# Global queries of four heads in the partitions of one tile, and transposes and products with V of neighbouring units in one gap

## The chip, the cores and the metric

The kernel runs on one core of a Trainium2 chip. The metric is device time in microseconds (us). Engines are named as the profile names them: PE (TensorE; PEld is its loading of weights), DVE (VectorE), ACT (ScalarE), POOL (GpSimd) and SP (which issues the DMAs).

## What is computed

An attention with local and global tokens, and a gated feed-forward layer on its output. There are 8 batches, 8 heads, 512 local and 32 global tokens, and 64 columns a head; the feed-forward has 512 columns in and out and 1536 hidden ones.

```python
k_all, v_all = concat([k_g, k_l]), concat([v_g, v_l])
out_g = softmax(q_g @ k_all.T / 8) @ v_all            # global queries see all keys
s_ll = where(abs(i - j) <= 32, q_l @ k_l.T / 8, -1e9) # local ones a window
out_l = softmax(concat([q_l @ k_g.T / 8, s_ll])) @ concat([v_g, v_l])
x = concat([out_g, out_l]).reshape(4352, 512)         # heads side by side
y = (sigmoid(x @ w_gate) * (x @ w_val)) @ w_out
```

The feed-forward weights arrive as float64 words and are converted on the chip.

## The kernel before

The tokens go through in chunks. Chunks 0 and 1 are halves of batch 0 (256 local tokens each), chunks 2 to 8 are one batch each (512 local tokens); a last feed-forward chunk takes the 256 global tokens of all batches. While the feed-forward of one chunk runs on PE, the attention of the next is put between its matmuls; from chunk 2's feed-forward on this is a steady alternation; beside the feed-forward of chunk 8 and of the global tokens no attention runs.

Numbers are kept to near float32: a float32 operand is split into two float32r parts, and a product takes three passes (high by high, low by high, high by low). In `ffn_stream` one step handles 128 hidden columns f of a chunk: twelve matmuls of 512 tokens into `bank_g`, twelve into `bank_v`, and twelve of the step before into four output banks `bank_o`. A **tick** is four such matmuls, so a step has nine ticks and a chunk 108. After each tick the generator yields, and all events of the queue that are due are issued; an event's number in the list (-1 to 9) decides between events of one tick. The recording layer may then still move instructions within each engine.

`att_events` puts the attention of a chunk in the queue. A head has two local units of two 128-query blocks each (one in the half chunks), and, where the chunk has global queries (chunks 1 to 8), one global unit of its 32 queries: 64 global units in all. Units follow each other every `PER` = 4 ticks (1.1 in chunk 1, 3 in chunk 2), and a unit has four stages, at 0, 3, 6 and 9 ticks of its start (scaled by a quarter of the spacing in chunks 1 and 2):

- stage 0: scores on PE into `bank_x` (L225; global: L299 into `bank_x`, L301 into `bank_y`), masking or maximum on DVE, exponential on ACT (L240; global: L308, L309);
- stage 1: reciprocal of the sum and scaling on DVE (into `p_buf`, or `pg_buf` for global units);
- stage 2: transposes on PE into `bank_y` (L254: four of 128x128; global L317: five of 32x128), a copy on ACT and the low part on DVE (`pt` L264; `ptg` L324);
- stage 3: products with V on PE into `bank_x` (L280 and L281; global L330), then copy on ACT, sum on DVE, sum on POOL into `x32` (L285; global `xg32`, L337).

`x_split` then makes the two parts of the feed-forward's input. Chunks 0 and 1 and the first four heads of chunk 2 are *native*: q, k and v stay float32 and are not split. All of `bank_g`, `bank_v`, `bank_x` and `bank_y` rotate through four of the eight banks of PSUM (`tag="att", bufs=4`). `vhl` holds V of a head in two parts, in two buffers. In ticks -2 to 45 the weights are converted (`convert`: DVE, ACT and POOL), beside the two half chunks and the first heads of chunk 2.

Of the kernel before, what the change touches and what calls it, by code (L numbers as in the profile page):

```python
# [17 lines left out]
P = 128  # L18
# [26 lines left out]
# the engines that share a kind of operation in turn: v(ector), s(calar)  # L45
# [9 lines left out]
def kernel(ctx, tc, qk, v, w_gate, w_val, w_out, out_l, out_g):  # L55
# [21 lines left out]
    # window column c < 96 stands for key c - 32, c >= 128 for key c - 64  # L77
    # (relative to the block's first query); the columns between are global
# [15 lines left out]
    pg = const.tile([32, 5 * P], F32, name="pg_buf")  # L94
# [24 lines left out]
    def convert(i, hi, lo):  # L119
        """The two float32r parts of a float64 [128, KT or 1, n] block, given as words."""  # L120
        src = w_src[i]
        t, n = src.shape[1], src.shape[2] // 2
        st, v = (o[i % len(o)].rearrange("p (t n) -> p t n", t=t) for o in conv_bufs)
        words = st.rearrange("p t (n two) -> p t n two", two=2)
        low, high = words[:, :, :, 0], words[:, :, :, 1]
        vf, hf = v.bitcast(F32), high.bitcast(F32)
        with tc.issue_after(anchor[0].ins) if i < 3 else nullcontext():
            nc.vector.tensor_scalar(v, high, 0x80000000, None, op0=ALU.bitwise_and)
# [6 lines left out]
            nc.vector.scalar_tensor_tensor(v, low, 29, v, op0=ALU.logical_shift_right, op1=ALU.bitwise_or)  # L135
            nc.vector.scalar_tensor_tensor(v, high, 3, v, op0=ALU.logical_shift_left, op1=ALU.bitwise_or)
# [35 lines left out]
    def load_v(T):  # L172
        c, n = T["wins"], T["n"]
        if T["native"]:
            nw = c.stop
            ng = 16 // nw
            if T["h"] % ng == 0:
                t = spl.tile([P, ng, nw, D], F32, name="v_nat", tag="vhl")
                nc.sync.dma_start(t, v[n:n + ng, :, c].rearrange("n p j d -> p n j d"))
                T["group"]["v"] = t  # L180
# [19 lines left out]
    def split_v(T):  # L200
# [3 lines left out]
        vhl = spl.tile([P, 8, 2 * D], F32R, name="vhl")  # L204
# [11 lines left out]
    def local_unit(T, blocks, x32s, h, col0):  # L216
# [35 lines left out]
        for i in range(2):  # L252
            for t in range(2):
                nc.tensor.transpose(pt_ps[:, 2 * i + t], pb[:, i, t * P:(t + 1) * P], ident)  # L254
        if nat:
# [31 lines left out]
    def global_unit(T, b, h):  # L287
# [3 lines left out]
        prow, kt = 64 * (h % 2), h // 2  # L291
        qg = ks[0][:, QK - SG - q0:QK - q0]
        sa = ps.tile([32, 4, P], F32, name="bank_x", tag="att", bufs=4)
        sb = ps.tile([32, 32], F32, name="bank_y", tag="att", bufs=4)
        for half in range(2):
# [4 lines left out]
        for t, (src, k0) in enumerate(zip(ks, k0s)):  # L300
            nc.tensor.matmul(sb, qg, src[:, k0 + 96:k0 + 128], start=t == 0, stop=t == last)  # L301
        mg = small.tile([32, 4], F32, name="mg")
        saf = sa.rearrange("p a c -> p (a c)")
        nc.vector.tensor_reduce(mg[:, 0:1], saf, axis=AX.X, op=ALU.max)
        nc.vector.tensor_reduce(mg[:, 1:2], sb, axis=AX.X, op=ALU.max)
        nc.vector.tensor_scalar(mg[:, 2:3], mg[:, 0:1], mg[:, 1:2], -0.125, op0=ALU.max, op1=ALU.mult)
        sg = small.tile([32, 2], F32, name="sg")
        nc.scalar.activation(pg[:, 0:512], saf, AF.Exp, bias=mg[:, 2:3], scale=0.125, accum_out=sg[:, 0:1])  # L308
        nc.scalar.activation(pg[:, 544:576], sb, AF.Exp, bias=mg[:, 2:3], scale=0.125, accum_out=sg[:, 1:2])  # L309
        yield  # L310
        nc.vector.tensor_scalar(mg[:, 3:4], sg[:, 0:1], sg[:, 1:2], 1e-9, op0=ALU.add, op1=ALU.add)
        nc.vector.reciprocal(mg[:, 3:4], mg[:, 3:4])
        scaled(0, pg[:, 0:576], pg[:, 0:576], mg[:, 3:4])
        yield
        pt_ps = ps.tile([P, 5, 32], F32, name="bank_y", tag="att", bufs=4)
        for j in range(5):
            nc.tensor.transpose(pt_ps[:, j], pg[:, j * P:(j + 1) * P], ident[0:32, 0:32])  # L317
        if nat:
            pt = att.tile([P, 5, 32], F32, name="ptg_nat", tag="ptg", bufs=1)
            nc.scalar.copy(pt, pt_ps)  # L320
        else:
            pt = att.tile([P, 5, 64], F32R, name="ptg", bufs=1)
            nc.scalar.copy(pt[:, :, 0:32], pt_ps)
            nc.vector.tensor_tensor(pt[:, :, 32:64], pt_ps, pt[:, :, 0:32].bitcast(F32), op=ALU.subtract)  # L324
        yield
        vt = T["v"]
        xg = xg32[prow:prow + 64, kt, b * SG:(b + 1) * SG]
        o_ps = ps.tile([64, 32] if nat else [P, 64], F32, name="bank_x", tag="att", bufs=4)
        for j in range(5):
            nc.tensor.matmul(o_ps, vt[:, (VM + VS)[j], :], pt[:, j, :], start=j == 0, stop=j == 4)  # L330
        if nat:
            nc.scalar.copy(xg, o_ps)
            return
        y = att.tile([64, 64], F32, name="y", bufs=1)
        nc.scalar.copy(y, o_ps[64:128])
        nc.vector.tensor_tensor(y, o_ps[0:64], y, op=ALU.add)
        nc.gpsimd.tensor_tensor(xg, y[:, 0:32], y[:, 32:64], op=ALU.add)  # L337

# [70 lines left out]
    # ---- driver: attention of the next chunk runs between the matmul groups  # L409
    def att_events(ci, start, per, tail=0):  # L410
        """(tick, order, thunk) of all attention work for chunk ci."""
# [19 lines left out]
        def adv(h, i):  # L431
            if (h, i) not in gens:
                gens[h, i] = (local_unit(heads[h], blocks[2 * i:2 * i + 2], x32s, h, 2 * i * P) if i < nu
                              else global_unit(heads[h], b, h))
# [3 lines left out]
        for h in range(NH):  # L438
# [30 lines left out]
    # the first two half chunks share the steps in which the weights are converted  # L469
# [7 lines left out]
    # events on the feed-forward's clock: one tick is four 512-token matmuls  # L477
# [23 lines left out]
    queue.sort(key=lambda e: e[:2])  # L501
# [9 lines left out]
def host_layout(inputs):  # L511
# [11 lines left out]
    for j in range(4):  # L523
# [7 lines left out]
        ve[:, VS[j], 32:64] = vg  # L531
        if j < 3:
# [31 lines left out]
```

## Time and profile before

| | |
|---|---|
| median of three runs | 1266.6 us (1265.78 to 1267.1) |
| profiled execution, its span | 1265.6 us |
| mean granted clock of PE | 0.986 |
| attention of chunk 0 before the first feed-forward matmul | to 49.7 us |
| outputs of the two half chunks | from 272.2 us |
| outputs of chunks 2 to 6 start at | 418.4, 557.6, 696.8, 835.9, 975.1 us |
| outputs of chunks 7, 8 and of the global tokens start at | 1113.6, 1211.3, 1260.9 us |

The times of outputs show the steady part: 139.1 to 139.2 us from chunk to chunk with attention beside the feed-forward, 97.7 us without. In the profile's lines `bank_x<-pt,vhl` reads "written from"; the number behind it is that of instructions, then busy us and mean ns of one, then the engine's idle time before them with what ended it. Matmuls overlap, so what a block of them costs is read from start to start in the timeline, not from the mean.

### The profile page before, as it was taken

The page shows a single profiled execution, that of the slowest core. Times are in us where ns is not written, and L with a number is a line of the kernel's source. Part 1 is how long each engine was busy: PE and PEld are TensorE (multiplying, and loading weights), DVE is VectorE, ACT ScalarE, POOL GpSimd, SP SyncE. Part 2 cuts the span into 40 slices and gives each one's busy share as a digit, 9 for nine tenths or more (in the row PEclk, how much of TensorE's full clock was granted, in tenths as well). Part 3 has the DMA queues.
Part 4 walks back from the last instruction along what each step waited for, and adds up shares of the span by engine and source line. Part 5 has one row for each costly group of instructions (what it writes and reads, how often), then busy time and mean ns, then how long its engine had stood idle before and what let it go on. Part 6 is the DMA issues. An engine that isn't in the chain of part 4 may idle for free.

```text
span 1265.6 us, 20474 instructions
## 1 busy us (share of the span) xinstructions
PE 1221.5 (97%) x6820; PEld 994.1 (79%) x6820; DVE 877.6 (69%) x2433; ACT 783.3 (62%) x1899; POOL 570.6 (45%) x573
## 2 busy tenths in 40 slices
PE   5899989999999999999999999999999999999998
PEld 4676768788788877888788877888788877888897
DVE  4797976757877777857876778767775787632232
ACT  4586766756666666666666667756765766532233
POOL 1444554545555355545555455535554555311111
PEclk9698999999999999999999999999999999999999
DMA  5576864333333333333333423343334332122143
GB/s 198 197 259 225 254 191 145 92 121 99 92 107 98 115 99 108 91 121 108 107 92 107 126 78 107 109 127 111 92 86 126 116 92 87 44 90 67 67 133 117
DMA packets 59497, 151.90 MB, mean 120 GB/s; under 512 B 6144, under 2 KB 19456, under 8 KB 59392
## 3 DMA queue, kind: packets, MB, share of 16 engines
q1 hardware_dynamic: 59392, 150.59, 38.9%
q8 instruction: 54, 0.88, 0.3%
q14 instruction: 51, 0.42, 0.1%
HBM read 135.36 MB, written 15.20 MB: 119 GB/s over the span
## 4 chain that ended last, share of the span: by engine, by line
PE 77%; DVE 13%; ACT 5%; issue 3%; POOL 1%; DMA 1%; SPq 0%; POOLq 0%; DVEq 0%; ACTq 0%
PE bank_g L362 20%; PE bank_v L362 19%; PE bank_o L396 19%; PE bank_x L225 5%; PE bank_y L254 4%; DVE p_buf L213 3%; DVE th L378 2%; PE bank_y L317 2%; PE bank_x L330 2%; PE bank_x L280 2%; PE bank_x L299 2%; PE bank_x L281 1%; DVE pg_buf L213 1%; ACT s_sb L240 1%; DVE pt L264 1%
## 5 line engine op out<-in xcount | busy, mean ns | idle before, releaser
L362 PE MATMUL bank_g<-xt,wg 128*128 128x512 f32 (+1 forms) x1440 | 340.3, 371 | 1.8 <-DVE th L380 1.8
L362 PE MATMUL bank_v<-xt,wv 128*128 128x512 f32 (+1 forms) x1440 | 332.6, 368 | 3.0 <-DVE pt L264 2.7
L396 PE MATMUL bank_o<-wo,hh 128*128 128x512 f32 x1224 | 334.0, 404 | 0.8 <-ACT hh L382 0.4
L362 PEld LDWEIGHTS bank_g<-xt,wg 128*128 128x128 f32 x1440 | 238.6, 192 | 41.6 <-issue 3.4
L362 PEld LDWEIGHTS bank_v<-xt,wv 128*128 128x128 f32 x1440 | 237.8, 190 | 40.7 <-PE bank_y L301 3.1
L396 PEld LDWEIGHTS bank_o<-wo,hh 128*128 128x128 f32 x1224 | 214.1, 189 | 38.9 <-ACT hh L382 1.2
L383 POOL TENSOR_TENSOR hh<-th,hh 128x512 fp32r<-128x512 f32 (+1 forms) x120 | 137.6, 1147 | 199.7 <-ACT hh L382 198.8
L240 ACT ACTIVATE s_sb<-s_sb,nm 128x224 f32<-128x224 f32 x240 | 113.8, 475 | 143.1 <-DVE nm L237 142.0
L213 DVE TENSOR_SCALAR p_buf<-s_sb,r 128x128 f32<-128x128 f32 (+1 forms) x443 | 151.8, 386 | 4.2 <-PE bank_y L254 0.4
L375 DVE TENSOR_SCALAR mn<-bank_g 128x512 f32<-128x512 f32 (+1 forms) x108 | 67.3, 623 | 110.7 <-ACT th L370 109.3
L378 DVE SCALAR_TENSOR_TENSOR th<-th,mn 128x512 f32<-128x512 f32 (+1 forms) x120 | 101.5, 846 | 59.0 <-ACT mn L376 52.7
L285 POOL TENSOR_TENSOR x<-t 64x256 f32<-64x256 f32 x104 | 76.4, 734 | 142.8 <-DVE t L284 138.7
L194 POOL TENSOR_TENSOR kl<-qk_raw,qk_hi 128x704 fp32r<-128x704 f32 x52 | 88.4, 1701 | 114.8 <-ACT qk_hi L193 114.8
L370 ACT ACTIVATE th<-bank_g 128x512 f32<-128x512 f32 (+1 forms) x120 | 63.5, 529 | 97.7 <-PE bank_g L362 96.1
L382 ACT CAST hh<-th 128x512 fp32r<-128x512 f32 (+1 forms) x120 | 66.5, 554 | 68.1 <-DVE th L380 67.3
L237 DVE CUSTOM_DVE_ANT_0 s_sb<-bank_x,masks 128x224 f32<-128x224 f32 x240 | 83.8, 381 | 12.7 <-PE bank_x L225 8.4
L254 PE MATMUL bank_y<-ident,p_buf 128*128 128x128 f32 x496 | 80.1, 282 | 10.8 <-DVE p_buf L213 6.6
L196 POOL TENSOR_TENSOR qk_hi<-qk_raw,qk_hi 64x256 fp32r<-64x256 f32 x104 | 87.7, 863 | 4.1
L254 PEld LDWEIGHTS bank_y<-ident,p_buf 128*128 128x128 f32 x496 | 60.9, 143 | 32.5 <-ACT pg_buf L308 6.6
L243 DVE TENSOR_SCALAR r<-sm 128x2 f32<-128x2 f32 x128 | 29.3, 229 | 75.5 <-ACT s_sb L240 74.2
L193 ACT CAST qk_hi<-qk_raw 128x1248 fp32r<-128x1248 f32 x52 | 64.1, 1233 | 22.2 <-PE bank_y L301 22.1
L380 DVE TENSOR_TENSOR th<-bank_v,th 128x512 f32<-128x512 f32 (+1 forms) x120 | 72.4, 604 | 5.1 <-PE bank_v L362 1.3
(109 smaller groups left out, 1985.9 us busy)
## 6 DMA issues: line engine op xcount, KB each, us to landing
wo<-wo_dram SPq DMA_DIRECT2D x116, 512.0 KB, 3.5
qk_raw<-in_qk_dram SPq DMA_DIRECT2D x104, 312.0 KB, 4.4
v_raw<-in_v_dram SPq DMA_DIRECT2D x52, 256.0 KB, 2.6
out_dram<-ob SPq DMA_DIRECT2D x34, 256.0 KB, 3.0
xt<-in_w_gate_dram SPq DMA_DIRECT2D x12, 512.0 KB, 4.5
xt<-in_w_val_dram SPq DMA_DIRECT2D x12, 512.0 KB, 4.4
xt<-in_w_out_dram SPq DMA_DIRECT2D x12, 512.0 KB, 4.9
v_nat<-in_v_dram SPq DMA_DIRECT2D x8, 512.0 KB, 5.5
```

The source lines that it names most:

```text
L194: nc.gpsimd.tensor_tensor(kl, t[:, K0:Q1], hi[:, K0:Q1].bitcast(F32), op=ALU.subtract)
L196: nc.gpsimd.tensor_tensor(hi[64:128, r], t[64:128, r], hi[64:128, r].bitcast(F32), op=ALU.subtract)
L213: nc.vector.tensor_scalar(out, in_, by, None, op0=ALU.mult)
L237: anchor[0] = nc.vector.tensor_tensor_reduce(out=s_sb[:, i], in0=s_ps[:, i, 0:WIN], in1=masks[:, m], scale=-0.125, scalar=3.0e38, op0=ALU. ...
L240: nc.scalar.activation(s_sb[:, i], s_sb[:, i], AF.Exp, bias=nm[:, i:i + 1], scale=-1.0, accum_out=sm[:, i:i + 1])
L254: nc.tensor.transpose(pt_ps[:, 2 * i + t], pb[:, i, t * P:(t + 1) * P], ident)
L285: nc.gpsimd.tensor_tensor(dst, t0[:, :, 0], t0[:, :, 1], op=ALU.add)
L362: nc.tensor.matmul(acc, w[a][:, t, fs], xt[:, c, t, x0:x0 + ntok], start=n == 0, stop=n == 11)
L378: nc.vector.scalar_tensor_tensor(th, th, 1.0, mn, op0=ALU.add, op1=ALU.mult)
L380: nc.vector.tensor_tensor(th, acc, th, op=ALU.mult)
L383: nc.gpsimd.tensor_tensor(hh[:, 1, 0:ntok], th, hh[:, 0, 0:ntok].bitcast(F32), op=ALU.subtract)
L396: nc.tensor.matmul(o_ps[t], ph[:, a, t * P:(t + 1) * P], pwo[:, c], start=f2 == 0 and i == 0, stop=f2 == NF - 1 and i == 2)
```

## The change

Four things change.

- **Global units of four heads share one tile.** `pg` has 128 partitions instead of 32. At each head's stage 0 ACT copies the raw scores (32x512 and 32x32) into rows 32(h mod 4) of `pg`. The first three heads of four end there. At the fourth, one maximum, one exponential, one scaling over 128 partitions x 544 columns, five transposes of 128x128 (into two banks), one copy and one low part for each bank, and then, in one stage, the 20 products with V (five of each head, as before) into one bank, with one sum for all four. The 32 global keys move from columns 544 to 575 to columns 96 to 127, ahead of the local ones, so the host puts V of the global tokens in the matching rows of a window of V that was empty there.
- **Stages.** The copies after the transposes become a stage of their own, and products with V come at 6 + `PER` ticks instead of 9. So they fall on the tick of the transposes of the next unit. `STAGES` now has pairs of ticks and orders: on one tick the transposes (2) go first, then the products of the unit before (3), then the copies of the new transposes (4). `x_split` follows one tick later.
- **Buffers of V.** `vhl` and `v_nat` have five buffers instead of two, since V of four heads is kept until the group's products. The room for software-issued DMAs is set to 512 bytes, which makes place for it; all DMAs of the kernel are issued by SP.
- Event times are rounded to six digits before they are sorted, and the scores against the global keys are issued ahead of those against the local ones.

PE, one local unit to the next, in the steady part, before (`pt` and `vhl` are the products with V, `p_buf` the transposes, `bank_g` the feed-forward):

```order
L301 MATMUL bank_y<-kl,qk_hi 32x32
L362 MATMUL bank_g<-xt,wg_111 128x512 x4
L280 MATMUL bank_x<-pt,vhl 128x256
L281 MATMUL bank_x<-pt,vhl 128x256
L280 MATMUL bank_x<-pt,vhl 128x256
L281 MATMUL bank_x<-pt,vhl 128x256
L362 MATMUL bank_g<-xt,wg_112 128x512 x4
L254 MATMUL bank_y<-ident,p_buf 128x128 x4
L362 MATMUL bank_g<-xt,wg_111 128x512 x4
```

and in the changed kernel, at a place of the same kind:

```order
L308 MATMUL bank_x<-kl,qk_hi 32x4x64
L379 MATMUL bank_g<-xt,wg_111 128x512 x4
L379 MATMUL bank_g<-xt,wg_112 128x512 x4
L261 MATMUL bank_y<-ident,p_buf 128x128 x4
L288 MATMUL bank_x<-pt,vhl 128x256
L289 MATMUL bank_x<-pt,vhl 128x256
L288 MATMUL bank_x<-pt,vhl 128x256
L289 MATMUL bank_x<-pt,vhl 128x256
L379 MATMUL bank_g<-xt,wg_111 128x512 x4
```

The products have moved behind the transposes of the next unit, and two ticks of the feed-forward now stand together ahead of them.

PE at the transposes of a global unit (`pg_buf`), before, of one head:

```order
L280 MATMUL bank_x<-pt,vhl 128x256
L281 MATMUL bank_x<-pt,vhl 128x256
L362 MATMUL bank_v<-xt,wv_113 128x512 x4
L317 MATMUL bank_y<-ident,pg_buf 128x32 x5
L396 MATMUL bank_o_4958<-wo,hh 128x512
```

and in the changed kernel, of four heads:

```order
L379 MATMUL bank_v<-xt,wv_113 128x512 x4
L329 MATMUL bank_y<-ident,pg_buf 128x128
L329 MATMUL bank_x<-ident,pg_buf 128x128 x4
L288 MATMUL bank_x<-pt,vhl 128x256
L289 MATMUL bank_x<-pt,vhl 128x256
L288 MATMUL bank_x<-pt,vhl 128x256
L289 MATMUL bank_x<-pt,vhl 128x256
L413 MATMUL bank_o_6115<-wo,hh 128x512
```

The five transposes have 128 output columns instead of 32 and take two banks, and the products of the local unit before them claim a third in the same gap.

DVE at a global unit, before, of one head (`mg` and `sg` are the maxima and sums, `ptg` the transposed rows):

```order
L304 TENSOR_REDUCE mg<-bank_x 32x1
L305 TENSOR_REDUCE mg<-bank_y 32x1
L306 TENSOR_SCALAR mg<-mg 32x1
L311 TENSOR_SCALAR mg<-sg 32x1
L312 RECIPROCAL mg<-mg 32x1
L213 TENSOR_SCALAR pg_buf<-pg_buf,mg 32x576
```

and in the changed kernel, of four heads:

```order
L317 TENSOR_REDUCE mg<-pg_buf 128x1
L318 TENSOR_SCALAR mg<-mg 128x1
L321 TENSOR_SCALAR mg<-sg 128x1
L322 RECIPROCAL mg<-mg 128x1
L220 TENSOR_SCALAR pg_buf<-pg_buf,mg 128x544
```

One reduce over SBUF stands in place of two over PSUM, and the sequence comes once for four heads.

```diff
+GH = P // SG
+G0 = P - SG
+VBUFS = GH + 1
-STAGES = (0, 3, 6, 9)
+STAGES = ((0, 2), (3, 2), (6, 2), (6, 4), (6 + PER, 3))
...
-    pg = const.tile([32, 5 * P], F32, name="pg_buf")
+    pg = const.tile([P, 5 * P], F32, name="pg_buf")
...
-        vhl = spl.tile([P, 8, 2 * D], F32R, name="vhl")
+        vhl = spl.tile([P, 8, 2 * D], F32R, name="vhl", bufs=VBUFS)
...
                 nc.tensor.transpose(pt_ps[:, 2 * i + t], pb[:, i, t * P:(t + 1) * P], ident)
+        yield
         if nat:
...
-    def global_unit(T, b, h):
+    def global_unit(T, b, h, heads):
...
+        rows = slice(SG * (h % GH), SG * (h % GH + 1))
+        nc.scalar.copy(pg[rows, P:], sa)
+        nc.scalar.copy(pg[rows, G0:P], sb)
+        if h % GH < GH - 1:
+            return
+        keys = pg[:, G0:]
...
+        nc.vector.tensor_reduce(mg[:, 0:1], keys, axis=AX.X, op=ALU.max)
+        nc.vector.tensor_scalar(mg[:, 0:1], mg[:, 0:1], -0.125, None, op0=ALU.mult)
+        nc.scalar.activation(keys, keys, AF.Exp, bias=mg[:, 0:1], scale=0.125, accum_out=sg)
+        yield
+        nc.vector.tensor_scalar_add(mg[:, 1:2], sg, 1e-9)
+        nc.vector.reciprocal(mg[:, 1:2], mg[:, 1:2])
+        scaled(0, keys, keys, mg[:, 1:2])
+        yield
+        banks = []
+        for bank, c0, c1 in (("bank_y", 0, 1), ("bank_x", 1, 5)):
+            pt_ps = ps.tile([P, c1 - c0, P], F32, name=bank, tag="att", bufs=4)
+            for c in range(c0, c1):
+                nc.tensor.transpose(pt_ps[:, c - c0], pg[:, c * P:(c + 1) * P], ident)
+            banks.append((pt_ps, c0, c1))
+        yield
+        pt = att.tile([P, 5, P if nat else 2 * P], F32 if nat else F32R, name="ptg", tag="ptg", bufs=1)
+        for pt_ps, c0, c1 in banks:
+            nc.scalar.copy(pt[:, c0:c1, 0:P], pt_ps)
+            if not nat:
+                nc.vector.tensor_tensor(pt[:, c0:c1, P:], pt_ps, pt[:, c0:c1, 0:P].bitcast(F32), op=ALU.subtract)
+        yield
+        o_ps = ps.tile([64, GH, 32] if nat else [P, GH, 2, 32], F32, name="bank_x", tag="att", bufs=4)
+        for g in range(GH):
+            vt = heads[h - GH + 1 + g]["v"]
+            for i, c in enumerate((1, 2, 3, 4, 0)):
+                p_c = pt[:, c].rearrange("p (a g q) -> p a g q", g=GH, q=SG)[:, :, g]
+                nc.tensor.matmul(o_ps[:, g], vt[:, (VS[3:] + VM)[c], :], p_c, start=i == 0, stop=i == 4)
...
-                for o in STAGES:
-                    ev.append((t0 + sc * o, 2, lambda h=h, i=i: adv(h, i)))
+                for o, order in STAGES:
+                    ev.append((t0 + sc * o, order, lambda h=h, i=i: adv(h, i)))
...
-                ev.append((base + (nu - 1) * per + sc * STAGES[-1] + 0.5, 3,
+                ev.append((base + (nu - 1) * per + sc * STAGES[-1][0] + 0.5, 3,
...
-    nc = bacc.Bacc("TRN2", target_bir_lowering=False, num_devices=1)
+    nc = bacc.Bacc("TRN2", target_bir_lowering=False, num_devices=1, dynamic_dma_scratch_size=512)
```

More of the change, by code (lines that the diff above doesn't have):

```diff
@@ L294, in global_unit @@
         sb = ps.tile([32, 32], F32, name="bank_y", tag="att", bufs=4)
+        for t, (src, k0) in enumerate(zip(ks, k0s)):
+            nc.tensor.matmul(sb, qg, src[:, k0 + 96:k0 + 128], start=t == 0, stop=t == last)
         for half in range(2):
@@ L325, in global_unit @@
[L325 to L332, printed above, removed]
+        banks = []
[4 more added lines that the diff above has]
+            banks.append((pt_ps, c0, c1))
@@ L333, in global_unit @@
+        k0 = (h + 1 - GH) // 2
+        xg = [xg32[64 * i:64 * i + 64, k0:k0 + GH // 2, b * SG:(b + 1) * SG] for i in range(2)]
+        if nat:
+            for i in range(2):
+                nc.scalar.copy(xg[i], o_ps[:, i::2])
             return
-        y = att.tile([64, 64], F32, name="y", bufs=1)
+        y = att.tile([64, GH, 2, 32], F32, name="y", tag="t0", bufs=1)
         nc.scalar.copy(y, o_ps[64:128])
         nc.vector.tensor_tensor(y, o_ps[0:64], y, op=ALU.add)
-        nc.gpsimd.tensor_tensor(xg, y[:, 0:32], y[:, 32:64], op=ALU.add)
+        for i in range(2):
+            nc.gpsimd.tensor_tensor(xg[i], y[:, i::2, 0], y[:, i::2, 1], op=ALU.add)
@@ L433, in adv @@
                 gens[h, i] = (local_unit(heads[h], blocks[2 * i:2 * i + 2], x32s, h, 2 * i * P) if i < nu
[L434 removed]
+                              else global_unit(heads[h], b, h, heads))
             next(gens[h, i], None)
```

31 lines of the change are left out of this document (6 added, 25 removed).

## The prediction

> **What bounds the kernel now.** I read the page's head first, then the busy time by stretches, then TensorE's timeline inside one stretch.
>
> ```profile
> span 1265.6 us, 20474 instructions
> ...
> PE 1221.5 (97%) x6820; PEld 994.1 (79%) x6820; DVE 877.6 (69%) x2433; ACT 783.3 (62%) x1899; POOL 570.6 (45%) x573
> ```
>
> ```profile
> core 0: us, PE busy (x) PEld busy (x) DVE busy (x) ACT busy (x) POOL busy (x), PEclk, DMA share, GB/s
> 10.00:50.00 40.00, 31.96 (x127) 21.30 (x124) 27.48 (x101) 21.09 (x59) 9.51 (x8) 0.82 0.50 176
> 50.00:115.00 65.00, 62.42 (x385) 46.60 (x385) 55.51 (x160) 48.49 (x151) 28.03 (x23) 0.90 0.75 245
> 115.00:180.00 65.00, 58.03 (x375) 45.99 (x375) 61.33 (x143) 45.08 (x127) 33.55 (x27) 0.96 0.74 233
> 180.00:272.00 92.00, 87.67 (x625) 76.10 (x625) 61.08 (x187) 62.95 (x177) 48.43 (x52) 0.99 0.39 117
> 280.00:1115.00 835.00, 826.76 (x4512) 673.34 (x4511) 626.22 (x1758) 550.17 (x1280) 425.42 (x429) 1.00 0.35 102
> 1115.00:1265.00 150.00, 145.79 (x765) 123.41 (x763) 40.84 (x73) 49.08 (x96) 22.91 (x23) 1.00 0.30 99
> ```
>
> There are two regimes. From 280 to 1115 us (attention of chunks 3 to 8 beside the feed-forward) TensorE is busy for 827 of 835 us at full clock, while DVE and ACT have a quarter and a third of their time free: a piece of PE's program is worth its whole length there. From 50 to 180 us (weights converted beside attention of chunks 1 and 2) DVE is busy for 116.8 of 130 us, and PE, at a granted clock of 0.90 and 0.96, is not the only bound: its "busy" contains matmuls that wait. After 1115 us there is no attention, and the change touches nothing.
>
> **The transposes of global queries.** PE's timeline, before:
>
> ```profile
> 710.62 1.10 PE L362 MATMUL bank_g<-xt,wg 128*128 128x512 f32 x4
> 711.64 0.49 PE L317 MATMUL bank_y<-ident,pg_buf 32*128 32x32 f32 x5
> 712.06 2.13 PE L362 MATMUL bank_v<-xt,wv 128*128 128x512 f32 x8
> 714.03 0.27 PE L225 MATMUL bank_x<-qk_hi 128*128 128x224 f32 x1
> ...
> 753.54 0.36 PE L280 MATMUL bank_x<-pt,vhl 128*128 128x256 f32 x1 [0.52 <-DVE pt L264]
> ...
> 754.09 1.09 PE L396 MATMUL bank_o<-wo,hh 128*128 128x512 f32 x4
> 755.02 0.60 PE L254 MATMUL bank_y<-ident,p_buf 128*128 128x128 f32 x4
> 755.37 1.17 PE L396 MATMUL bank_o<-wo,hh 128*128 128x512 f32 x4
> 756.38 1.10 PE L362 MATMUL bank_g<-xt,wg 128*128 128x512 f32 x4
> ```
>
> Four feed-forward matmuls take 755.02 - 754.09 = 0.93 us from start to start. From 755.02 to 756.38 lie four transposes and four such matmuls: 1.36 - 0.93 = 0.43 us, 0.108 each. From 710.62 to 714.03 lie twelve matmuls and the five small transposes of one head: 3.41 - 2.79 = 0.62 us. The change makes five 128x128 transposes (the form just priced at 0.108, so 0.54 us) for four heads, in place of four blocks of 0.62. That is 1.94 us less a group. There are 64 units, so 16 groups: 64 x 0.62 - 16 x 0.54 = **31.0 us**, of which 12 groups (23.3 us) lie in the full-PE stretch. The scores and the products with V keep number and form (five products of 64 columns a head), so they cost the same.
>
> ```profile
> L254 PEld LDWEIGHTS bank_y<-ident,p_buf 128*128 128x128 f32 x496 | 60.9, 143 | 32.5 <-ACT pg_buf L308 6.6 <-issue 6.2 <-DVE p_buf L213 3.9
> L317 PEld LDWEIGHTS bank_y<-ident,pg_buf 32*128 32x128 f32 x320 | 24.3, 136 | 24.7 <-issue 11.1 <-DVE nm L237 4.8 <-PE bank_o L396 3.6
> ```
>
> These rows say that loading 32x128 takes as long (136 ns) as 128x128 (143). The Trainium skill ("TensorE: Matmul & The Clock Gate", LDWEIGHTS) has the rule behind it: the load goes by columns, P / 1.2 ns, whatever the rows; if loads alone paced transposes, by my estimate from its figure (107 ns) the saving would be 48 blocks x 0.53 = 26 us; the trace agrees on the equal loads, and the measured 0.62 stands.
>
> **The merged gap.** Transposes of a unit and the products with V of the one before it now follow each other on PE; their count is the same, and after the transposes the next block starts as late as a feed-forward block does now (inside the 0.43), so the merge itself costs nothing and saves nothing. What it changes is waiting: the products come four ticks and two attention blocks after the copy of their operand, instead of three ticks and one.
>
> ```profile
> PE bank_x L280 <- DVE pt L264: 3.6, 9, 0.5
> PE bank_v L362 <- DVE pt L264: 2.7, 6, 0.5
> PE bank_y L317 <- DVE pg_buf L213: 1.2, 6, 0.2
> PE bank_x L280 <- DVE mg L312: 0.5, 3, 0.2
> ```
>
> These are all of PE's waits from 280 to 1115 us: 8.0 us. The first and last are what the longer distance removes; the second is a bank of PSUM not yet free, and may stay. I take 4 us, with ends at 8 gained and 8 lost (as many new waits as there are now, since two or three of the four rotating banks are now claimed in one gap).
>
> **VectorE and ScalarE.**
>
> ```profile
> L304 DVE TENSOR_REDUCE mg<-bank_x 32x1 f32<-32x512 f32 x64 | 42.9, 671 | 7.4 <-PE bank_x L299 4.9 <-PE bank_y L301 2.4
> L305 DVE TENSOR_REDUCE mg<-bank_y 32x1 f32<-32x32 f32 x64 | 10.8, 169 | 0.0
> L306 DVE TENSOR_SCALAR mg<-mg 32x1 f32<-32x1 f32 x64 | 12.8, 200 | 1.9
> L311 DVE TENSOR_SCALAR mg<-sg 32x1 f32<-32x1 f32 x64 | 12.8, 199 | 47.3 <-ACT pg_buf L309 47.3
> L312 DVE RECIPROCAL mg<-mg 32x1 f32<-32x1 f32 x64 | 9.5, 148 | 1.4
> L213 DVE TENSOR_SCALAR pg_buf<-pg_buf,mg 32x576 f32<-32x576 f32 x64 | 56.5, 883 | 1.9
> L324 DVE TENSOR_TENSOR ptg<-bank_y,ptg 128x160 fp32r<-128x160 f32 x52 | 15.9, 305 | 0.0
> L336 DVE TENSOR_TENSOR y<-bank_x,y 64x64 f32<-64x64 f32 x52 | 10.9, 209 | 18.6 <-ACT y L335 17.5
> L264 DVE TENSOR_TENSOR pt<-bank_y,pt 128x512 fp32r<-128x512 f32 x104 | 70.1, 674 | 0.0
> ...
> L308 ACT ACTIVATE pg_buf<-bank_x,mg 32x512 f32<-32x512 f32 x64 | 43.2, 674 | 15.7 <-DVE mg L306 15.4
> L309 ACT ACTIVATE pg_buf<-bank_y,mg 32x32 f32<-32x32 f32 x64 | 16.8, 263 | 0.0
> L283 ACT COPY t<-bank_x 64x512 f32<-64x512 f32 x104 | 60.6, 583 | 5.4 <-PE bank_x L281 3.0
> L335 ACT COPY y<-bank_x 64x64 f32<-64x64 f32 x52 | 10.8, 208 | 9.5 <-PE bank_x L330 8.4
> ```
>
> A head's softmax now costs DVE 671 + 169 + 200 + 199 + 148 + 883 = 2.27 us, with the split of its operand and the sum of the result (305 + 209) 2.78. A group of four will cost about 0.7 (one reduce of 544 columns), 0.2, 0.2, 0.15 and 0.85 (544 of 576 columns), 2.1 us; with splits of 512 and 128 columns (0.67 + 0.27) and the sum of 256 (about 0.4), 3.44. Native heads, 12 of 64, have neither split nor sum. DVE loses 3 x (9.1 - 2.1) + 13 x (11.1 - 3.4) = **121 us** of work. ACT gives up two exponentials a head (0.674 + 0.263, and their read-outs of the sum) for two copies (0.58 + 0.2) and one exponential a group: a little less work. In the full-PE stretch both are cover already, and their change is worth only the shorter waits above. The new wait at a group's end (copies, reduce, exponential, scaling before five transposes six ticks later) adds 0.8 us of copies to the chain, against 5.6 us of six ticks; nothing else is queued behind it on DVE for longer than now.
>
> **The start, 50 to 180 us.** Here lie the eight global units of chunk 1 and three of chunk 2 (one every nine ticks from tick 29, while conversions run to tick 46). PE's part: 11 x 0.62 - 2 x 0.54 = 5.7 us. DVE's part: 11 x 2.27 - 2 x 2.1 = 20.8 us of its 116.8.
>
> ```profile
> by line: PE bank_g L362 10.9%; issue 8.4%; PE bank_x L225 7.4%; PE bank_v L362 7.1%; DVE xt L128 6.4%; DVE xt L135 6.4%; DVE xt L136 5.9%; PE bank_x L299 5.3%; DVE pg_buf L213 4.2%; PE bank_y L254 4.0%; PE bank_o L396 4.0%; DVE p_buf L213 2
> ```
>
> That is the chain of work of this stretch. If DVE set its length throughout, 20.8 / 0.9 = 23 us would go; if DVE is hidden, only PE's 5.7. The chain runs through both, with the scaling of global rows on it for 4.2% of 130 = 5.5 us. I take PE's part and this one, **11 us**, ends 5.7 and 23. The transfers are the next in line: 0.75 of their time is used, so a stretch shorter by over a quarter would meet them. From 180 to 272 us: five blocks less, two new ones, 5 x 0.62 - 2 x 0.54 = 2.0 us, and a us of waits, **3 us** (2 to 5). Chunk 0 (10 to 50 us) has no global units; its products come one unit later on PE, which is idle for much of that time (clock 0.82): nothing, within 2 us either way. More buffers for V and their earlier loads, and moving the splits of x by one tick, lie beside PE's work: nothing.
>
> **Sum.** 23.3 + 4 + 11 + 3 = 41 us off the profiled span of 1265.6: 1224. The median of the runs is 1 us above that span, so **1225 us**.
>
> **Rivals.**
> (a) Only PE's own work goes, and the start stays bound by conversions: 1265.6 - 31 + 1, 1235, with some new waits up to 1243. For it: half the start's chain is not DVE's global work. Against: DVE is at 90% there.
> (b) The start follows DVE: 23 instead of 11, and all waits go: 1207 to 1216. Against: transfers at 0.75, and conversions spread by ticks.
>
> ```profile
> L370 ACT ACTIVATE th<-bank_g 128x512 f32<-128x512 f32 x84 | 49.9, 594 | 78.1 <-PE bank_g L362 77.5
> L375 DVE TENSOR_SCALAR mn<-bank_g 128x512 f32<-128x512 f32 x84 | 57.3, 682 | 80.6 <-ACT th L370 79.1
> ```
>
> (c) The other side: the merged gap claims banks that are not yet evicted. A gate block's eviction takes ACT and DVE at least 1.28 us (594 + 682 ns), and at a group's end the transposes (two banks) and products fill about 1.0 us before the next block needs one. If each of the 128 merged gaps (one per local unit) waited, it decides from 41 / 128 = 0.32 us a gap; at the 0.52 us seen at 753.54 the time is 1225 + 67 = 1292. Against: only 8 us of waits now, at similar distances, and DVE, which frees most banks, loses work. The Trainium skill ("Perfetto Trace Analysis", Optimization Strategy) says that the same gap repeating on the saturated engine can mean too few buffers; now no such gap shows.
> (d) The removed work comes back as waits elsewhere, so that the change hardly shows: 1243 to 1264, or no change.
>
> **Chances.** The forecast (1216 to 1234) 0.50, (a) 0.20, (b) 0.17, (d) 0.05 faster and 0.03 the same, (c) 0.05. Faster by over 0.2% (what a measurement here can tell from no change) 0.92, within it 0.03, slower 0.05. The range takes in (a) and (b): 1206 to 1243.
>
> **What would show it.** After: 80 transposes of pg_buf at 0.108 us from start to start, PE's waits from 280 us on at or under 8 us, the stretch between two chunks' outputs 3.9 us plus some waits shorter than now, DVE's busy time near 757 us, and the start's conversions ending about 11 us earlier. Wrong would be: feed-forward matmuls that wait for a bank after each merged gap, or a start that ends where it did.

## The result, and the profile after

The changed kernel takes 1286.29 us (median of four runs, 1282.14 to 1288.99) where the kernel before takes 1266.55 (1265.78 to 1267.1): ratio 1.0141, 95% interval 1.0111 to 1.0172. It is slower, where 1225 was forecast.

The page of the kernel after, its head:

```profile
span 1284.4 us, 19421 instructions
...
PE 1202.5 (94%) x6580; PEld 988.2 (77%) x6580; DVE 768.4 (60%) x2064; ACT 761.0 (59%) x1726; POOL 555.7 (43%) x547
```

DVE gave up 109 us of work, where 121 was forecast, the transposes are fewer, and PE's share has fallen from 97% to 94%: the saturated engine is less saturated. Busy time by stretches after, then the rows at which the outputs of the half chunks and of chunk 7 start (timeline; start, duration, engine, line):

```profile
core 0: us, PE busy (x) PEld busy (x) DVE busy (x) ACT busy (x) POOL busy (x), PEclk, DMA share, GB/s
10.00:50.00 40.00, 31.65 (x104) 20.32 (x101) 22.79 (x97) 17.34 (x52) 5.20 (x5) 1.00 0.53 180
50.00:115.00 65.00, 59.31 (x359) 42.96 (x358) 52.48 (x123) 48.64 (x136) 29.79 (x25) 0.95 0.71 240
115.00:180.00 65.00, 55.99 (x326) 44.85 (x324) 53.47 (x115) 38.83 (x104) 28.26 (x23) 0.87 0.65 209
...
280.00:1115.00 835.00, 795.07 (x4258) 656.58 (x4257) 532.75 (x1466) 525.18 (x1136) 404.97 (x393) 0.99 0.34 101
```

```profile
277.45 0.68 DVE L421 TENSOR_SCALAR ob<-bank_o 128x512 f32<-128x512 f32 x1
...
1132.68 0.69 DVE L421 TENSOR_SCALAR ob<-bank_o 128x512 f32<-128x512 f32 x1 [0.89 <-PE bank_o L413]
```

Before, these outputs started at 272.2 and 1113.6 us. So the steady part went from 841.4 to 855.2 us (13.8 more, where 27 less was forecast), the part ahead of it is 5.2 us longer (14 less was forecast), and the tail is the same (152.0 and 151.7). Of the 5.2 us, 4.8 lie in chunk 0: the first feed-forward matmul starts at 54.5 us instead of 49.7. They may not be the change's: beside the experiments the kernel before ran in 1264.8 to 1268.3 us 51 times (mean clock 0.983 to 0.989) and in 1271.2 to 1272.5 us 18 times (0.992 to 0.994), and a higher clock is what goes with the late chunk 0 here (1.00 from 10 to 50 us, 0.82 before), but no trace of the longer executions was kept.

PE's waits after, 280 to 1115 us, the longest four of 39.8 us in all (8.0 before):

```profile
PE bank_v L379 <- DVE pt L272: 13.7, 12, 1.2
PE bank_x L308 <- DVE mn L392: 8.5, 6, 3.1
PE bank_y L261 <- DVE p_buf L220: 5.5, 12, 0.7
PE bank_x L232 <- DVE t L292: 4.5, 6, 0.8
```

Counts of 6 and 12 say that a wait stands at one or two fixed places of each of the six steady chunks, not at every merged gap. DVE is named in all four, though it is busy for 533 of 835 us. So the question is what stood ahead of `pt`, `mn`, `p_buf` and `t` in the queues of engines that have a third of their time free.

PE's own work comes first. Its timeline after, at one group (transposes, then products):

```profile
484.20 0.27 PE L329 MATMUL bank_y<-ident,pg_buf 128*128 128x128 f32 x1
484.31 0.60 PE L329 MATMUL bank_x<-ident,pg_buf 128*128 128x128 f32 x4
484.66 0.36 PE L288 MATMUL bank_x<-pt,vhl 128*128 128x256 f32 x1
...
490.36 2.40 PE L343 MATMUL bank_x<-ptg,vhl 128*128 128x64 f32 x20
492.59 1.19 PE L413 MATMUL bank_o<-wo,hh 128*128 128x512 f32 x4
```

and the products of one head before:

```profile
591.93 0.64 PE L330 MATMUL bank_x<-ptg,vhl 128*128 128x64 f32 x5
592.40 1.18 PE L362 MATMUL bank_g<-xt,wg 128*128 128x512 f32 x4
```

Five transposes cost 484.66 - 484.20 = 0.46 us, as forecast. But a group's 20 products take 492.59 - 490.36 = 2.23 (the median of the twelve blocks is 2.19), and four blocks of five took 4 x 0.47 = 1.88: 0.35 more. Over the 48 steady blocks before, the second product of a block started 29 ns after the first and each later one 110; in the block of twenty, 19 pay 110. Likewise the 0.62 taken for a head's small transposes was a long one: the median over the 48 blocks is 0.51 (0.42 from the first to what follows, and 0.09 on the matmul ahead). By these prices a group saves 4 x 0.51 - 0.46 - 0.35 = 1.2 us, and twelve save 15, not 23.3.

The steady part: 15 us less work and 39.8 - 8.0 = 31.8 more waits make 16.8 more; 13.8 were measured. The sum leaves out the clock. Before, it is 1.00 in the whole steady part; after, three stretches of 3.41 us run at half clock, from 698.2, 858.6 and 984.9 us. Most of the first, as a window of the trace:

```profile
698.00:701.20 3.20, 3.20 (x10) 2.48 (x9) 0.42 (x1) 0.39 (x2) 0.73 (x3) 0.53 0.28 87
```

At half the pace they cost some 5 us (an estimate: half of 3 x 3.41). So PE's own work must have fallen by more than 15 us. The clean case is e8 below, which has the same grouping with the old stages and a clock of 1.00 throughout: its steady part less its waits of PE is 847.0 - 34.9 = 812.1 us, against 841.4 - 8.0 = 833.4 before, 21 us less. As a total the forecast's 23.3 was near; the pieces priced above give 15, and where the other 6 lie was not followed up.

### The profile page after: what moved, and what is told of

Same layout as the page of the kernel before. It is cut to its first block, busy times and chain, and to the rows that moved or that the text cites. A ratio compares the mean times of both kernels' runs of the same rounds, so it can differ in the third digit from the quotient of the medians.

```text
span 1284.4 us, 19421 instructions
## 1 busy us (share of the span) xinstructions
PE 1202.5 (94%) x6580; PEld 988.2 (77%) x6580; DVE 768.4 (60%) x2064; ACT 761.0 (59%) x1726; POOL 555.7 (43%) x547
## 4 chain that ended last, share of the span: by engine, by line
PE 63%; DVE 13%; ACT 9%; DMA 6%; POOL 5%; issue 4%; SPq 0%; POOLq 0%; DVEq 0%; ACTq 0%
PE bank_v L379 18%; PE bank_g L379 16%; PE bank_o L413 14%; PE bank_x L232 4%; DMA v_raw<-in_v_dram 4%; PE bank_y L261 4%; DVE p_buf L220 3%; ACT s_sb L247 3%; POOL vhl L213 2%; PE bank_x L308 2%; POOL hh L400 1%; PE bank_x L343 1%; PE bank_x L289 1%; PE bank_x L288 1%; DVE th L395 1%
## 5 line engine op out<-in xcount | busy, mean ns | idle before, releaser
L379 PE MATMUL bank_v<-xt,wv 128*128 128x512 f32 (+1 forms) x1440 | 328.6, 367 | 17.4 <-DVE pt L272 13.7
L379 PE MATMUL bank_g<-xt,wg 128*128 128x512 f32 (+1 forms) x1440 | 333.1, 369 | 4.3 <-ACT xt L361 4.3
L413 PE MATMUL bank_o<-wo,hh 128*128 128x512 f32 x1224 | 321.8, 398 | 5.3 <-ACT hh L399 2.5
L379 PEld LDWEIGHTS bank_g<-xt,wg 128*128 128x128 f32 x1440 | 243.9, 192 | 50.8 <-ACT xt L361 6.9
L413 PEld LDWEIGHTS bank_o<-wo,hh 128*128 128x128 f32 x1224 | 218.9, 189 | 50.8 <-POOL hh L400 4.4
L220 DVE TENSOR_SCALAR p_buf<-s_sb,r 128x128 f32<-128x128 f32 (+1 forms) x443 | 145.1, 377 | 6.5
L292 DVE TENSOR_TENSOR t<-bank_x,t 64x512 f32<-64x512 f32 x104 | 70.5, 678 | 108.9 <-ACT t L291 108.8
L395 DVE SCALAR_TENSOR_TENSOR th<-th,mn 128x512 f32<-128x512 f32 (+1 forms) x120 | 88.0, 734 | 65.5 <-ACT mn L393 49.4
L261 PE MATMUL bank_y<-ident,p_buf 128*128 128x128 f32 x496 | 82.8, 282 | 23.6 <-DVE p_buf L220 16.6
L213 POOL TENSOR_TENSOR vhl<-v_raw,vhl 128x512 fp32r<-128x512 f32 x52 | 67.7, 1302 | 64.6 <-ACT vhl L212 56.4
L250 DVE TENSOR_SCALAR r<-sm 128x2 f32<-128x2 f32 x128 | 34.4, 268 | 88.4 <-ACT s_sb L247 86.0
L203 POOL TENSOR_TENSOR qk_hi<-qk_raw,qk_hi 64x256 fp32r<-64x256 f32 x104 | 79.7, 787 | 4.1
```

The source lines that it names most:

```text
L203: nc.gpsimd.tensor_tensor(hi[64:128, r], t[64:128, r], hi[64:128, r].bitcast(F32), op=ALU.subtract)
L213: nc.gpsimd.tensor_tensor(vhl[:, :, D:2 * D], t, vhl[:, :, 0:D].bitcast(F32), op=ALU.subtract)
L220: nc.vector.tensor_scalar(out, in_, by, None, op0=ALU.mult)
L379: nc.tensor.matmul(acc, w[a][:, t, fs], xt[:, c, t, x0:x0 + ntok], start=n == 0, stop=n == 11)
L395: nc.vector.scalar_tensor_tensor(th, th, 1.0, mn, op0=ALU.add, op1=ALU.mult)
L413: nc.tensor.matmul(o_ps[t], ph[:, a, t * P:(t + 1) * P], pwo[:, c], start=f2 == 0 and i == 0, stop=f2 == NF - 1 and i == 2)
```

## The experiments

All ratios are to the kernel before, run on the same chip beside them. Line numbers of the grouped kernels are up to 6 above those of the changed kernel.

**e1: V's casts spread.** In the order of ACT's instructions before, some 20 rows lie between two casts of V (`vhl<-v_raw`; read-outs of sums are not counted); after, 81, 3, 6, 7, 53, 3, 4 and 4: with five buffers the recording layer issues a group's four casts together. `v_raw` has one buffer, so each cast stands on ACT until the next head's V has landed:

```profile
ACT vhl L212 <- DMA v_raw<-in_v_dram: 38.9, 31, 2.8
```

(waits of ACT after, 280 to 1115 us; no such row before). ACT's and DVE's timeline after, and the row of PE that waits at its end:

```profile
569.01 0.62 ACT L212 CAST vhl<-v_raw 128x512 fp32r<-128x512 f32 x1 [2.48 <-DMA v_raw<-in_v_dram]
...
570.48 0.58 ACT L387 ACTIVATE th<-bank_g 128x512 f32<-128x512 f32 x1
570.61 0.42 DVE L250 TENSOR_SCALAR r<-sm 128x2 f32<-128x2 f32 x1 [1.50 <-ACT s_sb L247]
...
572.36 0.67 DVE L392 TENSOR_SCALAR mn<-bank_g 128x512 f32<-128x512 f32 x1
...
573.09 0.31 PE L308 MATMUL bank_x<-qk_hi 128*32 128x256 f32 x1 [1.91 <-DVE mn L392]
```

ACT stood 2.48 us for the load. Behind it in line were two exponentials and the tanh of a gate block whose matmuls had ended by 568. DVE's `mn`, the other reader of that block, stood behind `r`, which waited 1.50 us for those exponentials, and behind an output copy that waited 0.66 us for its buffer. It came at 572.36, and PE waited 1.91 us for the bank. The edit queues a cast behind the last exponential:

```diff
+    last_exp = [None]
...
-        nc.scalar.copy(vhl[:, :, 0:D], t)
+        with tc.issue_after(last_exp[0].ins):
+            nc.scalar.copy(vhl[:, :, 0:D], t)
...
-            nc.scalar.activation(s_sb[:, i], s_sb[:, i], AF.Exp, bias=nm[:, i:i + 1], scale=-1.0,
+            last_exp[0] = nc.scalar.activation(s_sb[:, i], s_sb[:, i], AF.Exp, bias=nm[:, i:i + 1], scale=-1.0,
```

> The changed kernel, with each cast of V (vhl, on ACT) queued behind the exponential that was issued last at its event, so that the four casts of a group no longer stand within 3 to 7 instructions of each other in ACT's order (81, 3, 6, 7, 53, 3, 4, 4 apart in the changed kernel, 20, 19, 21, 19, 16, 31 before) but 16 to 27 apart. Theory V (ACT stands before bunched casts until V's single raw buffer is loaded again, and gate evictions behind it come late, so banks of PSUM come late): ACT's idle time before vhl casts falls from 42.6 to under 5 us and the time to 1225 to 1245 us. Rival B (three banks claimed in one merged gap are the cause): the waits of PE for DVE's evictions stay, 1275 to 1287 us.

Measured: 1276.24 us (1.0049, 1.0019 to 1.0079), 10 us less than after; 16 to 27 rows between casts, and no wait of ACT for `v_raw` left. So the bunch is real and half of the loss, but with it gone the kernel is still no faster than before: something else takes the gain. PE's longest wait in e1:

```profile
PE bank_v L381 <- DVE pt L274: 20.2, 12, 2.1
```

**e2, e3, e4: the parts alone.** e2 is the change with the old stages (no merged gap); e3 is the kernel before with the new stages alone; e4 is e2 with V's casts spread as in e1.

```diff
-STAGES = ((0, 2), (3, 2), (6, 2), (6, 4), (6 + PER, 3))
+STAGES = ((0, 2), (3, 2), (6, 2), (6, 2), (9, 2))
```

> The changed kernel with the stages of before (transposes and their copies at tick 6, products with V at tick 9), global queries still grouped by four. Theory V: the casts of V stay bunched (79, 4, 5, 8, 54, 2, 4, 4 apart), so the time stays at 1270 to 1290 us. Rival B: without the merged gap the grouping brings its 31 us of PE work, 1230 to 1240 us.

Measured: 1273.32 (1.0056, 1.003 to 1.0082).

> The kernel before with the new stages alone (copies as a stage, products with V on the tick of the next unit's transposes), global units head by head, two buffers of V. Theory V: no bunched casts (20, 18, 22, 19, 14, 33 apart), so within 1255 to 1270 us, near the kernel before at 1266.6. Rival B: the banks cost it what they cost the changed kernel over its saved work, 1290 us or more.

Measured: 1296.3 (1.0225, 1.0192 to 1.0258). Its outputs of the half chunks start 24 us later than before, its steady part is 847.0 us (841.4 before). The stretch of the conversions in e3:

```profile
50.00:115.00 65.00, 60.12 (x300) 44.28 (x299) 48.96 (x124) 39.70 (x119) 25.08 (x21) 0.76 0.62 204
115.00:180.00 65.00, 56.60 (x321) 44.58 (x320) 53.61 (x131) 38.95 (x116) 23.81 (x20) 0.82 0.67 223
```

PE did 300 matmuls there instead of 385, at a clock of 0.76 instead of 0.90. The changed kernel, with five buffers of V, loses much less at this place; whether the buffers are why was not tried.

> Grouping with the stages of before and with casts of V spread as in the first run. Theory V: 1228 to 1245 us, and against the first run it shows what the merged gap is worth by itself (0 to 8 us in favour of the merge). Rival B: 1230 to 1240 us as in the run with bunched casts, since casts do not matter to it.

Measured: 1267.41 (0.9999, 0.9981 to 1.0017). So the merge costs 9 us in the grouped kernel (e1 against e4), spreading the casts gives 6 there (e2 against e4), and grouping by itself gives nothing, although 15 us or more of PE's work are gone. Where the 9 us lie is less clear: of the 7.4 us between the profiled executions of e1 and e4, 5.3 are chunk 0's and 2.6 the steady part's (848.6 and 846.0 us). e4's waits of PE are 30.3 us, 14.5 of them `bank_v` behind `pt`, 12 times.

**e5, e6, e7: another place.** The step's boundary is where global scores and the next block claim banks, so attention was moved by a tick against the feed-forward: in e4 (e5), in e1 (e6) and in the kernel before (e7).

```diff
-HOLE = (8, 1)
+HOLE = (8, 2)
```

> The kernel of e4 with every attention stage after the eighth tick of a step one tick later (HOLE 2 in place of 1), nothing else. Theory P (place): the 22 us of PE waits that grouping added come from attention's banks being claimed at the tick at which the feed-forward's next block starts; then the 14.5 us of bank_v behind the pt copies and the 10.0 us of PV behind them fall by half or more, and the time is 1250 to 1258. Rival L (latency): the copies and POOL's low parts are as late wherever they stand, the waits move and stay 25 to 35 us in the steady part, 1263 to 1271.

> The kernel of e1 (the change with V's casts spread) with HOLE 2 in place of 1. Theory P: the 20.2 us of bank_v behind the pt copies fall under 8, 1258 to 1266. Rival L: the merged gap puts the copies of the transposes behind those of the predecessor's products wherever it stands, waits 25 us or more, 1271 to 1280.

> The kernel before with HOLE 2 alone, the control for the two others. If place is of use only to the grouped kernel: 1264 to 1270. If the shift helps any kernel: 1255 to 1262.

Measured: e5 1273.28 (1.0048, 1.0025 to 1.0072), e6 1289.39 (1.0178, 1.0143 to 1.0214), e7 1268.65 (1.0009, 0.9995 to 1.0023). Theory P falls: PE's waits were 39.2 us in e5 and 42.6 in e6, still behind `pt`, now at other matmuls (22.1 us at the products, 13.1 at the global scores in e5). The low part of `pt` is late wherever it is wanted.

**e8: POOL's low part of V on DVE.** The same 144th matmul of a chunk was read in the kernel before and in e4. Before (timeline; DVE, POOL and PE):

```profile
593.28 0.94 DVE L243 TENSOR_SCALAR r<-sm 128x2 f32<-128x2 f32 x1 [0.86 <-ACT s_sb L240]
...
594.33 0.20 DVE L336 TENSOR_TENSOR y<-bank_x,y 64x64 f32<-64x64 f32 x1
594.52 0.92 DVE L213 TENSOR_SCALAR p_buf<-s_sb,r 128x128 f32<-128x128 f32 x4
595.36 0.68 DVE L264 TENSOR_TENSOR pt<-bank_y,pt 128x512 fp32r<-128x512 f32 x1
...
592.89 1.30 POOL L383 TENSOR_TENSOR hh<-th,hh 128x512 fp32r<-128x512 f32 x1
594.67 0.25 POOL L337 TENSOR_TENSOR xg<-y 64x32 f32<-64x32 f32 x1 [0.48 <-DVE y L336]
595.00 1.38 POOL L206 TENSOR_TENSOR vhl<-v_raw,vhl 128x512 fp32r<-128x512 f32 x1
...
596.25 1.88 PE L362 MATMUL bank_v<-xt,wv 128*128 128x512 f32 x7
```

e4, the same place:

```profile
592.41 1.15 DVE L252 TENSOR_SCALAR r<-sm 128x2 f32<-128x2 f32 x1 [0.88 <-ACT s_sb L249]
...
593.87 1.63 DVE L222 TENSOR_SCALAR p_buf<-s_sb,r 128x128 f32<-128x128 f32 x4
595.43 0.67 DVE L274 TENSOR_TENSOR pt<-bank_y,pt 128x512 fp32r<-128x512 f32 x1
...
592.25 1.29 POOL L402 TENSOR_TENSOR hh<-th,hh 128x512 fp32r<-128x512 f32 x1
593.50 1.28 POOL L215 TENSOR_TENSOR vhl<-v_raw,vhl 128x512 fp32r<-128x512 f32 x1
...
596.25 0.93 PE L381 MATMUL bank_v<-xt,wv 128*128 128x512 f32 x3 [1.71 <-DVE pt L274]
```

Before, the sum of a head's global unit (`y`, then `xg`) held POOL's low part of V back to 595.00, when most of the scaling was done. With grouping `y` and `xg` come once for four heads; here they are gone, POOL starts at 593.50, and the four scalings take 1.63 us instead of 0.92. The low part of `pt` is behind them in DVE's line, and PE comes earlier by the products that it no longer has (the 0.47 us above): from its last score (594.26) to the block's start lie 1.99 us, against 0.03 before. e8 takes the one POOL operation away from there:

```diff
-        nc.gpsimd.tensor_tensor(vhl[:, :, D:2 * D], t, vhl[:, :, 0:D].bitcast(F32), op=ALU.subtract)
+        nc.vector.tensor_tensor(vhl[:, :, D:2 * D], t, vhl[:, :, 0:D].bitcast(F32), op=ALU.subtract)
```

> The kernel of e4 with V's low part subtracted on DVE in place of POOL, the same numbers. Theory C (contention): POOL's two low parts back to back stretch DVE's reciprocal and scaling beside them, and so the low part of pt that bank_v waits for; then v behind pt falls from 14.5 us under 8 and the time to 1255 to 1261. Rival: DVE has 32 more operations of some 0.5 us in line ahead of its copies, nothing gained or slower, 1265 to 1275.

Measured: 1269.35 (1.0013, 0.9994 to 1.0033): no change. DVE's rows in e8 at this place:

```profile
589.32 0.92 DVE L222 TENSOR_SCALAR p_buf<-s_sb,r 128x128 f32<-128x128 f32 x4
590.16 0.68 DVE L215 TENSOR_TENSOR vhl<-v_raw,vhl 128x512 fp32r<-128x512 f32 x1
590.76 0.68 DVE L274 TENSOR_TENSOR pt<-bank_y,pt 128x512 fp32r<-128x512 f32 x1
```

The scalings are back at 0.92, so POOL was what stretched them. But the moved operation takes 0.68 ahead of `pt`: `bank_v` still waits 12.5 us in all, and the products wait 16.6 us for `pt` where they waited 10.0 in e4. What is common to e4, e5 and e8 is that `pt`, which PE wants next, stands last in line.

**e9, e12: the order in the queues.** e9 queues DVE's four scalings of a unit behind the low part of the `pt` of the unit before, and ACT's cast of V behind the cast of `pt`; e12 does the first alone. No work is added. (In e9 the cast of `pt` also takes the place of the exponential in `last_exp`.)

```diff
             nc.scalar.copy(pt[:, 0], pt_ps)
-            nc.vector.tensor_tensor(pt[:, 1], pt_ps, pt[:, 0].bitcast(F32), op=ALU.subtract)
+            last_low[0] = nc.vector.tensor_tensor(pt[:, 1], pt_ps, pt[:, 0].bitcast(F32), op=ALU.subtract)
...
+        low = last_low[0]
...
-            scaled(nat, pb[:, i, 0:128].rearrange("p (a c) -> p a c", c=64), main, r[:, i:i + 1])
+            with (tc.issue_after(low.ins) if low is not None else nullcontext()):
+                scaled(nat, pb[:, i, 0:128].rearrange("p (a c) -> p a c", c=64), main, r[:, i:i + 1])
```

> The kernel of e4 with two orders fixed, no work added or removed: ACT's cast of V is queued behind the cast of pt, and DVE's four scalings of a unit behind the low part of the pt of the unit before. Theory Q (order in the queues): in e4 the low part of pt stands on DVE behind the reciprocal and the four scalings, 2.8 us that POOL stretches, so bank_v waits 1.97 and 1.0 us at the same two places of each chunk; with the low part ahead of them the 14.5 us of bank_v behind pt fall under 4, and the time is 1247 to 1257. Rival: the scalings are now late by as much and the transposes behind them wait instead, 1262 to 1270.

> The kernel of e9 with only DVE's order fixed (the four scalings behind the low part of pt); ACT's cast of V stands ahead of the cast of pt again, as in e4. If DVE's order is what e9 gained by: 1246 to 1254, bank_v behind pt under 6 us. If ACT's 0.6 us ahead of the cast of pt carried it: 1260 to 1268.

Measured: e9 1247.12 (0.9839, 0.9811 to 0.9868), e12 1246.27 (0.9829, 0.9799 to 0.9859; the median of three executions, since a fourth took 6486.79 us for a reason that is not known, and the trace kept is of that one, so e12's waits are not shown). Both are faster than the kernel before and 20 us faster than e4, and DVE's order carries all of it. e9 at the same place (DVE, then PE), and its longest two waits:

```profile
589.01 0.67 DVE L278 TENSOR_TENSOR pt<-bank_y,pt 128x512 fp32r<-128x512 f32 x1
589.60 1.34 DVE L223 TENSOR_SCALAR p_buf<-s_sb,r 128x128 f32<-128x128 f32 x4
...
589.74 1.20 PE L385 MATMUL bank_v<-xt,wv 128*128 128x512 f32 x4
```

```profile
PE bank_x L349 <- DVE ptg L342: 5.8, 11, 0.6
PE bank_v L385 <- DVE t L298: 2.9, 6, 0.5
```

`pt` is done by 589.68 and the block follows the last score at once. The scalings are still stretched by POOL, and nobody waits for them. PE's waits are 13.7 us in all, and the steady part is 826.8 us, 14.6 less than before: PE's saved work is seen at last, less 5.7 us of waits more than before and four stretches of 3.41 us at half clock.

**e10, e13: the merged gap with the orders mended.** e10 is e1 with e9's orders. e13 puts the predecessor's products ahead of the transposes in the gap, with the transposes' copies right behind them.

```diff
-STAGES = ((0, 2), (3, 2), (6, 2), (6, 4), (6 + PER, 3))
+STAGES = ((0, 2), (3, 2), (6, 2), (6, 2), (10, 1))
```

> The kernel of e1 (the change with V's casts spread) with the same two orders fixed. Theory Q: bank_v behind pt, 20.2 us now (2.4 and 1.5 us at the same two places of each chunk), falls under 8, 1258 to 1267. Rival: in the merged gap the copy of pt waits for the predecessor's products first, so the order on DVE changes nothing, 1272 to 1280.

> The kernel of e10 (merged gap, both orders fixed) with the predecessor's products ahead of the transposes in the gap, and the transposes' copies right behind them. Theory M: the 29 us between e9 and e10 come from the order inside the gap, where the copies of pt stand behind the products; then 1245 to 1260. Rival: two claims of banks in one gap cost it in either order, with waits of 25 us or more, 1268 to 1282.

Measured: e10 1276.61 (1.0068, 1.0042 to 1.0093), as e1; e13 1262.08 (0.9962, 0.9939 to 0.9985). Waits of PE in e10, then in e13:

```profile
PE bank_y L267 <- DVE p_buf L223: 9.4, 15, 1.4
...
PE bank_v L385 <- DVE pt L278: 1.4, 6, 0.5
```

```profile
PE bank_v L385 <- DVE mn L398: 8.2, 6, 1.4
...
PE bank_y L267 <- DVE p_buf L223: 0.3, 1, 0.3
```

In e10 the 20.2 us behind `pt` fell to 1.4, but the scalings now stand behind a `pt` whose copies follow the predecessor's products, and the transposes wait for them. With the products first that is gone, and half of the 29 us between e9 and e10. The steady parts of e9, e10 and e13 are 826.8, 849.6 and 839.1 us. The other half stays with the merge in either order; e13 still waits for banks that `mn` frees. Both theories were half right.

**e11: the order alone.** The kernel before with e12's edit.

> The kernel before with DVE's order fixed alone, the control: bank_v waits behind pt for 2.7 us there in all, so Theory Q gives 1262 to 1268; if the order helps any kernel, 1250 to 1260.

Measured: 1303.81 (1.0298, 1.027 to 1.0325), 37 us slower than before, and outside what was expected. Its longest wait of PE:

```profile
PE bank_y L259 <- ACT pg_buf L313: 10.7, 16, 2.7
```

There the transposes (`bank_y`) wait for a bank that ACT's exponential of the global scores frees late, 16 times. What in the order made that exponential late was not followed up. The order is thus no gain of its own: it fits the grouped kernel with the old stages.

## Why the prediction was wrong, by its steps

- **"The scores and the products with V keep number and form [...], so they cost the same"**: the products cost 0.35 us more a group, 4 us in the steady part. A block of small products behind a long matmul has one cheap start; four blocks have four, one block of twenty has one.
- **The transposes, 23.3 us**: the mechanism is right, the price of a block is off. 0.62 came from one clip, the median of 48 is 0.51, and with the products the priced pieces give 15 us. The total of PE's saved work is 21 us by e8, so that 23.3 came near it is partly luck.
- **"More buffers for V and their earlier loads ... nothing"**: failed, by 10 us (after against e1). The buffers let the recording layer put four casts in a row, and their loads, with one landing buffer, stood in ACT's line ahead of a gate block's tanh.
- **"The merge itself costs nothing"**: failed, by 29 us where the orders are mended (e10 against e9; their steady parts differ by 22.8), and by 9 without (e1 against e4). About half of the 29 hangs on which of the two goes first in the gap (e13); the rest is not settled.
- **"In the full-PE stretch both are cover already, and their change is worth only the shorter waits"**, 4 us gained with 8 lost at most: this is the step that sank the sum. Waits grew by 31.8 us. The free third of DVE's and ACT's time was read as cover, but each engine takes its operations one after the other (ACT stood 2.48 us for a load with a tanh behind it whose input was ready), and what counts is what stands ahead of the one operation that PE wants. That the order is the cause is shown for the grouped kernel with the old stages: e9 and e12, which move no work, take 20 us off. Why the order went wrong is argued from one place, where small operations that grouping removed (`y`, `xg`, a head's products) had kept PE, DVE and POOL apart; no run puts them back. The three stretches at half clock, some 5 us, were not in the sum either.
- **The start, 11 us**: not seen in the changed kernel. From the first feed-forward matmul to the half chunks' outputs it is 223.0 us against 222.5, with a clock of 0.95 and 0.87 instead of 0.90 and 0.96 in its two stretches. In the grouped kernels with the old stages (e2, e4, e5, e8, e9) it is 213.7 to 220.2 us, so 2 to 9 us do go where the gap is not merged. Chunk 0 ("nothing, within 2 us") lost 4.8 us. It ends late in e1 (54.4 us, merged), but also in e2 and e9 (52.7 and 53.2, not merged), and early in e4 (49.1, not merged) and e10 (48.6, merged); its cause stays open.
- **The rivals**: (c) had the side, not the mechanism. It wanted a wait at each of 128 gaps; there are a few long ones at fixed places. (d), work that comes back as waits, is what e4 shows, and its chance of 0.08 was far too low.

By the medians the cases line up: grouping with the orders mended 1247, without 1267, with the merged gap 1276, with V's casts bunched 1286. No run divides up the 22 us that are left between 1247 and the forecast. One more thing came with grouping and was not tried alone: `y` now takes the buffer of the local units' sum (`t0` in the code).

## What to carry to other kernels

Before work is taken from a saturated engine, look at each place where it will arrive earlier: what stands ahead of the operation that it wants, in the line of every engine of the chain, and not how busy those engines are. More buffers change the order of instructions as well as waits, so compare the order on each engine before and after, and spread what has bunched. A removed small operation may have kept two others apart.

## What the runs showed of the hardware

**DVE and POOL.** DVE's operation on `r` (128x2) took 1.15 us in e4, where the reciprocal of the same size behind it took 0.17. It ended at 593.56, POOL's low part of `hh` beside it at 592.25 + 1.29 = 593.54; before, 594.22 and 594.19. The scalings from SBUF took 0.92 us for four without POOL (e8) and 1.63 with it (e4; the first of them ends at 594.86, POOL's low part of V at 594.78), while the low part of `pt`, which reads PSUM and one SBUF tile, took its usual 0.67 in e9 with POOL's low part of V beside it (588.93 to 590.22). The Trainium skill ("SBUF — State Buffer", SBUF: two separate sides) says that a DVE operation in a two-port mode, or with two inputs in SBUF, and a POOL operation hold one pair of ports in turn, each for its whole instruction; these rows agree.

**The clock after a short wait.** In e1, after a wait of 2.12 us of PE for `bank_v`, the clock is at half; in e4 it is, too, behind a wait of only 0.49 us and a group's block of twenty small products (a window of e1, then a row of e4's timeline and a window of e4):

```profile
602.40:605.80 3.40, 3.38 (x8) 2.69 (x9) 1.16 (x2) 1.75 (x2) 1.06 (x1) 0.50 0.18 65
```

```profile
342.94 2.42 PE L345 MATMUL bank_x<-ptg,vhl 128*128 128x64 f32 x20 [0.49 <-DVE ptg L338]
...
345.65:349.06 3.41, 3.41 (x12) 2.71 (x11) 2.04 (x6) 0.70 (x2) 2.31 (x4) 0.50 0.33 82
```

In e1 eight matmuls ran at half clock, some 1.6 us lost on top of the wait. Five of its six waits of 2.1 us were followed so. In e4 none of the seven waits of 1.7 us was, but three of the blocks of twenty were; so were two in the kernel after. Before, with blocks of five, the steady part has no half clock; nor has e8, with blocks of twenty. So the length of a wait alone does not decide it, and blocks of twenty can go before it; what decides is open. The Trainium skill ("TensorE: Matmul & The Clock Gate", What's actually happening) gives one idle window of about 3.4 us as what halves the clock; here less idle time came before it.
